# A two-stage attention and FFN kernel: another release of the warm-up matmuls, and one transpose moved from TensorE to DMA

## The chip, the cores and the metric

The kernel runs on one core of one Trainium2 chip. The metric is the device time of one execution in microseconds (us). Three executions of the kernel before lie within 0.4% (317.28 to 318.57 us), so the question here is one of a few microseconds in 318. A profile is one execution of the same program; its span is some 2 us shorter than the time of the run it belongs to (315.7 against 317.68 us before).

## The reference, cut to what matters

```python
def _attn_ref(q, k, v):                      # 8 batches, 8 heads, 576 positions, 64 per head
    q_s = np.exp(q - q.max(-1, keepdims=True));  q_s = q_s / (q_s.sum(-1, keepdims=True) + 1e-09)
    k_s = np.exp(k - k.max(2, keepdims=True));   k_s = k_s / (k_s.sum(2, keepdims=True) + 1e-09)
    kv = np.einsum('bhsd,bhse->bhde', k_s, v)
    return np.einsum('bhsd,bhde->bhse', q_s, kv)

def _moe_ref(x, w_gate, w_val, w_out):       # x: 4608 x 512, d_ff = 1536
    g = x @ w_gate
    silu = g * (1.0 / (1.0 + np.exp(-g)))
    return (silu * (x @ w_val)) @ w_out
```

## The kernel before

All of it is one program with a list of instructions for each engine. The heads of a batch come in two groups, G = 0 and 1. The scaled q of a group must be transposed before the x matmuls (q times kv). There are two ways in the kernel: nine matmuls against an identity and two evictions, or one DMA transpose (the crossbar).

```python
def turn_pe(b, G, i):                        # TensorE: into a PSUM tile
    ...
    for t in range(t0, t1):
        nc.tensor.transpose(out=tp[:, ...], in_=s["qs"][:, t, :], identity=ident)

def turn_out(b, G, i, eng):                  # and out of it again, on ScalarE or VectorE
    copy(eng, s["qt"][:, t0:t1, :], s["tp", i]...)

def turn_dma(b, G):                          # DMA transpose, SyncE queue
    qt = s["qt"] = at.tile([128, T, 128], BF16, tag="qt", name="qt")
    nc.sync.dma_start_transpose(out=qt, in_=s["qs"].rearrange("p t c -> p (t c)"))
```

Batches 0 and 1 use TensorE, batches 2 to 7 the DMA transpose. The program starts with idle matmuls (`spin`) on zeros, only to keep TensorE busy. Then come batch 0's attention, its FFN units (`m_unit`), batch 1's attention with the first four output units (`o_mm`) between its steps, and the FFN in chunks:

```python
spin(9)
spin(7, first)                 # released by the first row sum of q
key_sum(0)
turn_pe(0, 0, 0); turn_pe(0, 0, 1)
...
spin(7)
kv_first(0)                    # needs v, loaded with a cast by a DMA of the GpSimd queue
... [batch 0 continues] ...
load_batch(1, w_dma[-3], by_group=True)      # SyncE queue: q, k, v of 576 KB each, two groups
load_batch(2)                                # right behind it on the same queue
for m in range(MT):
    m_unit(0, S, m, first=(m == 0))
... [exp of q and k, cast of v, sums of batch 1] ...
o_out(0, o_mm(0), nc.scalar)
o_out(1, o_mm(1), nc.scalar)
exp_of("k", 1, 1)
turn_pe(1, 0, 0); turn_pe(1, 0, 1)
turn_out(1, 0, 0, nc.scalar); turn_out(1, 0, 1, nc.scalar)
kv_one(1, 0)
scale_one(1, 0, (nc.vector, nc.vector))
norm_mul(1, 1)
p = o_mm(2)
x_one(1, 0)
o_out(2, p)
turn_pe(1, 1, 0); ...          # group 1 the same way, with o_mm(3)
```

The softmax here doesn't subtract the row's maximum and nothing guards it: scores larger than these inputs give would overflow.

## Time and profile before

| | before |
|---|---|
| time, median of 3 runs | 318.06 us (317.28 to 318.57) |
| span of the profiled run | 315.7 us |
| TensorE busy | 309.0 us, 98% |
| first FFN matmul of batch 0 | 15.40 us |
| first output unit (batch 1's attention begins) | 38.93 us |
| first FFN matmul of chunk 0 (batch 1's attention is done) | 53.11 us |

These are lines of the profile's page. A digit is the busy share of a fortieth of the span in tenths; PE is TensorE, PEld its weight loads, PEclk its granted clock, DVE VectorE, ACT ScalarE, POOL GpSimd.

```profile
PE 309.0 (98%) x1900; PEld 153.0 (48%) x1900; DVE 163.1 (52%) x277; ACT 147.5 (47%) x218; POOL 28.8 (9%) x36
PE   7999999999999999999999999999999999999994
PEclk9999999999999999999999999999999999999998
DMA  7999999179246808490639253944310202020124
```

TensorE has hardly a hole. DMA is full (the digit 9, busy for 90% or more) in the slices from 8 to 55 us: weights, then the loads of batches 1 and 2. What TensorE waited for in the whole span, by the list of waits (total, times, longest):

```profile
PE idle L388 <- DVE sel L367: 1.2, 1, 1.2
PE idle L388 <- DVE rs L138: 1.0, 1, 1.0
PE g_ps L298 <- ACT xt L111: 0.2, 1, 0.2
```

The start, from the timeline of TensorE (start, length, what, count, and in brackets the idle time before it and what ended it):

```profile
1.22 4.02 PE L388 MATMUL idle<-zero 128*128 128x512 bf16 x9 [1.22 <-DVE sel L367]
6.29 3.17 PE L388 MATMUL idle<-zero 128*128 128x512 bf16 x7 [1.05 <-DVE rs L138]
9.25 0.43 PE L397 MATMUL ks<-sel,ek 128*128 128x2 bf16 x9
13.67 0.68 PE L410 MATMUL kv<-v,ek 64*128 64x128 bf16 x18
15.40 0.45 PE L298 MATMUL g_ps<-xt,wg 128*128 128x320 bf16 x2
```

The seven idle matmuls before the key sums take 3.17 us: they start 0.43 us apart. Seven later ones, from 10.25 us, took 1.67 us: 0.22 us apart. These are called the slow and the fast pace here. The view by windows gives a granted clock of 1.00 in every microsecond from 1 to 12 us, so its column does not show this difference. The attention of batch 1, same view:

```profile
44.36 0.68 PE L166 MATMUL tp<-ident,qs 128*128 128x128 bf16 x9
45.60 2.76 PE L322 MATMUL o_ps<-wo,hr 128*128 128x512 bf16 x12
48.30 0.44 PE L220 MATMUL xp<-qt,kn 64*64 64x320 bf16 x8
50.04 2.76 PE L322 MATMUL o_ps<-wo,hr 128*128 128x512 bf16 x12
53.11 0.55 PE L298 MATMUL g_ps<-xt,wg 128*128 128x448 bf16 x2
```

Each of the two output units shown takes 2.7 us; the x matmuls follow without a wait. The twelve DMA transposes of later batches, by the view of the transposed tile:

```profile
L182 SPq DMA_TRANSPOSE qt<-qs x12: 1250/1338/1415, 61.9 to 221.0; - x12
DMA to landing us min/median/max: 3.2/3.3/4.4
```

### The profile page before, as it was taken

The numbers are of one execution on the slowest core, as the hardware profiler recorded it, in microseconds if no ns is written. First come the engines' busy times: TensorE is split into PE (matmuls) and PEld (weight loads), VectorE is DVE, ScalarE is ACT, GpSimd is POOL, SyncE is SP. The second block draws the span as 40 slices with busy tenths as digits, with TensorE's granted clock in tenths as the row PEclk, the third lists the DMA queues.
The fourth block names the chain that finished last, engine by engine and source line by source line (L and its number), as shares of the span: only waits on it lengthen the run. The fifth ranks groups of instructions, "written<-read, shape, count | busy, mean of one in ns | idle before, by whom it ended". The sixth has DMA issues, their size and how long they took to land.

```text
span 315.7 us, 4898 instructions
## 1 busy us (share of the span) xinstructions
PE 309.0 (98%) x1900; PEld 153.0 (48%) x1900; DVE 163.1 (52%) x277; ACT 147.5 (47%) x218; POOL 28.8 (9%) x36
## 2 busy tenths in 40 slices
PE   7999999999999999999999999999999999999994
PEld 2577744554444444544454444544444444444443
DVE  3744476684754566455835492639354333423421
ACT  5653487634673475447454637355743113312300
POOL 2930021101100020002000200020000000000000
PEclk9999999999999999999999999999999999999998
DMA  7999999179246808490639253944310202020124
GB/s 281 182 202 205 298 394 390 60 169 356 55 86 177 341 18 127 125 387 7 141 71 363 83 110 67 323 161 104 67 39 0 52 17 66 0 69 4 30 69 102
DMA packets 40088, 45.75 MB, mean 145 GB/s; under 512 B 17408, under 2 KB 23808, under 8 KB 40064
## 3 DMA queue, kind: packets, MB, share of 16 engines
q1 hardware_dynamic: 32480, 39.99, 42.4%
q0 software_dynamic: 7424, 5.31, 11.2%
q8 instruction: 15, 0.25, 0.3%
q10 hardware_dynamic: 160, 0.13, 0.2%
q14 instruction: 9, 0.07, 0.1%
HBM read 37.75 MB, written 9.44 MB: 149 GB/s over the span
## 4 chain that ended last, share of the span: by engine, by line
PE 94%; ACT 1%; DVE 1%; DMA 1%; issue 0%
PE g_ps L298 30%; PE u_ps L298 29%; PE o_ps L322 27%; PE kv L191 3%; PE idle L388 2%; DMA q<-in_q_dram 1%; PE xp L267 1%; PE tp L166 1%; PE o_ps L342 1%; DVE rs L138 1%; ACT eq L124 1%; PE xp L220 0%; DVE qs L152 0%; ACT L124 0%; PE kv L410 0%
## 5 line engine op out<-in xcount | busy, mean ns | idle before, releaser
L305 ACT ACTIVATE sg<-g_ps 128x512 bf16<-128x512 f32 (+2 forms) x120 | 65.0, 554 | 138.3 <-PE g_ps L298 131.2
L306 DVE TENSOR_TENSOR hr<-sg,u_ps 128x512 bf16<-128x512 bf16 (+2 forms) x120 | 74.4, 630 | 87.2 <-PE u_ps L298 82.3
L298 PE MATMUL g_ps<-xt,wg 128*128 128x512 bf16 (+2 forms) x480 | 111.8, 358 | 0.2 <-ACT xt L111 0.2
L298 PE MATMUL u_ps<-xt,wv 128*128 128x512 bf16 (+2 forms) x480 | 111.5, 358 | 0.0
L322 PE MATMUL o_ps<-wo,hr 128*128 128x512 bf16 x420 | 93.6, 379 | 0.0
L298 PEld LDWEIGHTS <-wv 128*128 128x128 bf16 x480 | 47.0, 98 | 46.4
L298 PEld LDWEIGHTS <-wg 128*128 128x128 bf16 x480 | 45.8, 98 | 45.1 <-issue 0.9
L322 PEld LDWEIGHTS <-hr 128*128 128x128 bf16 x420 | 40.9, 98 | 49.1
L113 DVE COPY o_sb<-o_ps 128x512 f32<-128x512 f32 x33 | 22.4, 680 | 39.2 <-PE o_ps L322 39.2
L127 POOL CAST vb<-v 128x1152 bf16<-128x1152 f32 x14 | 16.0, 1146 | 172.7 <-DMA v<-in_v_dram 113.4
L138 DVE TENSOR_REDUCE rs<-eq 128x18 f32<-128x1152 bf16 (+2 forms) x18 | 21.7, 1215 | 12.8 <-ACT eq L124 12.8
L152 DVE TENSOR_TENSOR qs<-eq,rr 128x1152 bf16<-128x1152 bf16 (+2 forms) x18 | 22.1, 1238 | 0.1
L124 ACT ACTIVATE eq<-q 128x1152 bf16<-128x1152 f32 (+2 forms) x18 | 18.1, 1051 | 4.1 <-DMA q<-in_q_dram 4.0
L124 ACT ACTIVATE ek<-k 128x1152 bf16<-128x1152 f32 x16 | 18.0, 1158 | 0.3 <-DMA k<-in_k_dram 0.2
L305 ACT ACT_TABLE_LOAD x12 | 15.4, 1283 | 0.2
L124 ACT ACT_TABLE_LOAD x11 | 14.1, 1283 | 0.2
L388 PE MATMUL idle<-zero 128*128 128x512 bf16 x26 | 9.7, 534 | 2.3 <-DVE sel L367 1.2
L191 PE MATMUL kv<-vb,ek 64*128 64x129 bf16 x252 | 8.7, 217 | 0.0
L191 PEld LDWEIGHTS <-ek 64*128 64x128 bf16 x252 | 7.3, 94 | 2.7 <-ACT sg L305 2.1
L275 ACT CAST xt<-xp 128x512 bf16<-128x512 f32 x12 | 6.4, 588 | 3.6 <-PE xp L267 3.6
L276 DVE CAST xt<-xp 128x512 bf16<-128x512 f32 x12 | 7.7, 683 | 0.0
L347 ACT COPY o_sb<-o_ps 128x128 f32<-128x128 f32 x2 | 0.5, 265 | 13.3 <-DVE o_sb L346 13.3
(44 smaller groups left out, 72.1 us busy)
## 6 DMA issues: line engine op xcount, KB each, us to landing
q<-in_q_dram SPq DMA_DIRECT2D x16, 576.0 KB, 5.2
k<-in_k_dram SPq DMA_DIRECT2D x16, 576.0 KB, 7.1
out_dram<-o_sb SPq DMA_DIRECT2D x70, 128.0 KB, 2.3
v<-in_v_dram SPq DMA_DIRECT2D x14, 576.0 KB, 8.8
wo<-in_moe_w_out_dram POOLq DMA_DIRECT2D x4, 384.0 KB, 15.3
wg<-in_moe_w_gate_dram POOLq DMA_DIRECT2D x3, 384.0 KB, 11.5
wv<-in_moe_w_val_dram POOLq DMA_DIRECT2D x3, 384.0 KB, 12.5
v<-in_v_dram POOLq DMA_DIRECT2D x2, 288.0 KB, 5.0
```

The costliest lines, as they stand in the source:

```text
L113: eng.tensor_copy(out=out, in_=in_)
L124: nc.scalar.activation(out=e[:, t0:t1], in_=src[:, t0:t1], func=AF.Exp)
L127: nc.gpsimd.tensor_copy(out=vbs[G][:, :, 0:128].rearrange("p t (h d) -> p t h d", d=64), in_=raw["v", b, G].rearrange("p h (t d) -> p t h ...
L138: i = nc.vector.reduce_sum(out=rs[:, 2 * t0:2 * t1], in_=eq2[:, 2 * t0:2 * t1, :], axis=mybir.AxisListType.X)
L152: nc.vector.tensor_mul(qs[:, t0:t1, :].rearrange("p t (h d) -> p (t h) d", d=64), eq2[:, 2 * t0:2 * t1, :], s["rr"][:, 2 * t0:2 * t1].to_b ...
L191: nc.tensor.matmul(out=kv[g][:, c:c + 129], lhsT=ek_of(b, G, g, t), rhs=vbs[G][r, t, 0:129], start=(t == 0), stop=(t == T - 1),)
L276: nc.vector.tensor_copy(out=xt[:, 2 * G + 1, c0:c0 + 512], in_=main[G][1])
L298: nc.tensor.matmul(out=gu[a][i][:, 0:w_], lhsT=(wg, wv)[a][:, kk, ms], rhs=xt[:, kk, c:c + w_], start=(kk == 0), stop=(kk == KT - 1),)
L305: nc.scalar.activation(out=sg[:, 0:w_], in_=g_ps[:, 0:w_], func=AF.Silu)
L306: nc.vector.tensor_mul(hr[:, m, r:r + w_], sg[:, 0:w_], u_ps[:, 0:w_])
L322: nc.tensor.matmul(out=o_ps, lhsT=hr[:, m, r0:r0 + 128], rhs=wo[:, m, :], start=(m == 0), stop=(m == MT - 1),)
L388: i = nc.tensor.matmul(out=idle, lhsT=zero[:, 0:128], rhs=zero, start=True, stop=True)
```

## The change: its intent and its diff

The intent is to bring TensorE to its fast pace sooner and to take nine transposes off TensorE and two evictions off ScalarE in batch 1, where everything waits on a chain. The transpose goes on ScalarE's DMA queue, because the SyncE queue is full of loads (in the profile before they run until about 55 us), and the x matmuls that need it move back by some steps.

```diff
-        spin(9)
-        spin(7, first)
+        spin(10)
+        for i in (0, 2, 4):          # steps: exp, exp, sum, sum, reciprocal of the first q
+            spin(3, steps[i])
 ...
-        spin(7)
+        spin(8)
 ...
         o_out(0, o_mm(0), nc.scalar)
+        turn_dma(1, 0, nc.scalar)
         o_out(1, o_mm(1), nc.scalar)
+        kv_one(1, 0)
         exp_of("k", 1, 1)
-        turn_pe(1, 0, 0)
-        turn_pe(1, 0, 1)
-        turn_out(1, 0, 0, nc.scalar)
-        turn_out(1, 0, 1, nc.scalar)
-        kv_one(1, 0)
-        scale_one(1, 0, (nc.vector, nc.vector))
         norm_mul(1, 1)
+        scale_one(1, 0, (nc.scalar, nc.scalar))
         p = o_mm(2)
-        x_one(1, 0)
-        o_out(2, p)
         turn_pe(1, 1, 0)
         ...
         kv_one(1, 1)
         scale_one(1, 1, (nc.vector, nc.vector))
+        x_one(1, 0)
+        o_out(2, p)
         p = o_mm(3)
```

(`exp_of` and `norm_sum` return their instructions, `turn_dma` takes an engine.)

More of the change, by code (lines that the diff above doesn't have):

```diff
@@ L122, in exp_of @@
         src = raw[what, b, G].rearrange("p h (t d) -> p t h d", d=64)
-        for t0, t1 in pieces:
-            nc.scalar.activation(out=e[:, t0:t1], in_=src[:, t0:t1], func=AF.Exp)
+        return [
+            nc.scalar.activation(out=e[:, t0:t1], in_=src[:, t0:t1], func=AF.Exp) for t0, t1 in pieces
+        ]
     def cast_v(b, G):
@@ L135, in norm_sum @@
         rs = at.tile([128, 2 * T], FP32, tag="rs", name="rs")
-        first = None
-        for t0, t1 in pieces:
-            i = nc.vector.reduce_sum(
+        done = [
+            nc.vector.reduce_sum(
                 out=rs[:, 2 * t0:2 * t1], in_=eq2[:, 2 * t0:2 * t1, :], axis=mybir.AxisListType.X
             )
-            first = first or i
+            for t0, t1 in pieces
+        ]
         rr = s["rr"] = at.tile([128, 2 * T], FP32, tag="rr", name="rr")
-        nc.vector.reciprocal(out=rr, in_=rs)
-        return first
+        done.append(nc.vector.reciprocal(out=rr, in_=rs))
+        return done
     def norm_mul(b, G, pieces=((0, T),)):
@@ L177, in turn_out, with turn_dma @@
         )
-    def turn_dma(b, G):
+    def turn_dma(b, G, eng=nc.sync):
         s = st[b, G]
         qt = s["qt"] = at.tile([128, T, 128], BF16, tag="qt", name="qt")
-        nc.sync.dma_start_transpose(out=qt, in_=s["qs"].rearrange("p t c -> p (t c)"))
+        eng.dma_start_transpose(out=qt, in_=s["qs"].rearrange("p t c -> p (t c)"))
     def ek_of(b, G, g, t):
@@ L371 @@
             nc.vector.memset(vb[:, :, 128:129], 1.0)
-        exp_of("q", 0, 0, BANKS)
+        steps = exp_of("q", 0, 0, BANKS)
         exp_of("k", 0, 0)
         exp_of("q", 0, 1, BANKS)
-        first = norm_sum(0, 0, BANKS)
+        steps += norm_sum(0, 0, BANKS)
         norm_mul(0, 0, BANKS)
```

## The prediction

> **What bounds the kernel.** TensorE. The page gives PE 309.0 us of a 315.7 us span (98%) and 94% of the chain of waits; the wait list names only 2.4 us of PE waiting, all before 54 us. So a gain can only come from PE work removed or from the first 54 us. Two places are bound otherwise: 5 to 39 us, where DMA runs at 90% or more, and 39 to 54 us (batch 1), where the chain passes through exp, sum and multiply of q.
>
> **Part 1, warm-up.** Before: nine idle matmuls from 1.22 us, start to start 0.427 us, then 1.05 us of idle PE, then seven more, still 0.427 us; fast ones (0.216 us) only from about 9.3 us. [...] After: 10+3+3+3, released at about 5.4, 6.2 and 7.1 us, leave no gap above about 0.3 us, so I expect fast matmuls from 5 to 8 us and key sums at about 7.9 instead of 9.25 us. The first FFN matmul then comes 0.5 to 1 us earlier than 15.40. But the weights do not: the third value-weight slice lands at about 22.2 us (read from the POOL issue that waits for it), and before uses it at 22.43. Most of the advance is given back in the fourth FFN unit as a new PE wait on DMA. Gain: 0.2 us, plus perhaps 0.2 in executions whose warm-up phase is bad.
>
> **Part 2, batch 1.** Removed: nine PE transposes (0.68 us), two ScalarE evictions (1.18 us); PE also need not wait 0.2 us for the scaled q at 44.3. Added on ScalarE: the issue of a DMA transpose (1.34 us by the twelve on SP) and two scalings (about 0.35 us each) moved from VectorE. Scaled q of group 1 is ready at about 47.5, its keys at 48.0. PE would reach the first x matmul of group 0 at about 48.9 us. The transpose is issued at about 45.0 us. Alone it lands 3.3 us after issue (48.3): then all is hidden, FFN chunk 0 starts 0.7 us sooner. But DMA is full (390 GB/s) until 55 us with loads of batches 1 and 2. [...] in this trace at 35.2 to 37 us, two queues shared and the older one's rest took about 3 times as long. A transpose is 1152 packets of 256 B, 1.45 us of transfer alone; shared with 2304 B packets I estimate 3 to 8 us, so landing at 49.5 to 55 us: PE would idle 0.5 to 6 us before the x matmuls, possibly followed by slow-clock matmuls. About 45% that it is hidden, 55% that it stalls.
>
> **Sum.** Hidden: -1 us. Stalled: 0 to +5 us. Predicted 318.3 us, 80% range 316.4 to 322.5; faster by over 2%: 1%, within: 94%, slower: 5%.
>
> **To check.** Warm-up: idle matmuls 0.216 us apart before 8 us; wait list with PE on the value weights at 21 to 22 us. Batch 1: x matmuls of group 0 wait for the DMA writing qt, or not; time from transpose issue to landing, 3.3 us or above 5; start of FFN chunk 0 against 53.11 us; ScalarE 1.3 us without work at 45 us.
>
> **What would make it wrong.** A transpose that lands late enough for the clock to fall; q, k loads of batch 2 pushed later by the transpose so that their exp delays the first silu (57.24 us); weight loads landing elsewhere than I read.

The sum came to -1 us if the transpose is hidden and 0 to +5 us if it stalls, together 318.3 us. Two terms stand as estimates alone: that a start without gaps brings the fast pace by 5 us, and that the transpose takes 3 to 8 us beside the loads.

## The result, and the profile after

The changed kernel takes 326.88 us (326.55 to 328.27, 4 runs) against 318.0 us: slower, ratio 1.0289, 95% interval 1.0253 to 1.0325. Ratios here are the mean time of one kernel's fast runs over that of the other's of the same rounds, so not quite the ratio of the medians quoted. The results are correct.

What TensorE waited for, in the changed kernel (two waits of 0.2 us left out):

```profile
PE xp L221 <- DMA qt<-qs: 7.7, 1, 7.7
PE idle L389 <- DVE sel L368: 1.2, 1, 1.2
PE tp L167 <- DVE qs L153: 0.8, 1, 0.8
PE kv L192 <- POOL vb L128: 0.3, 1, 0.3
```

A wait of 7.7 us is new: the x matmuls wait for the DMA that writes the transposed q. Its issue and landing in the view of that tile (ACTq is ScalarE's sequencer; the maximum of the landing times belongs to this one):

```profile
L183 ACTq DMA_TRANSPOSE qt<-qs x1: 1371/1371/1371, 43.9 to 43.9; - x1
DMA to landing us min/median/max: 3.2/3.3/12.7
```

12.7 us instead of 3.3. TensorE's timeline:

```profile
43.77 2.76 PE L323 MATMUL o_ps<-wo,hr 128*128 128x512 bf16 x11
47.30 0.68 PE L167 MATMUL tp<-ident,qs 128*128 128x128 bf16 x9 [0.77 <-DVE qs L153]
48.30 0.70 PE L192 MATMUL kv<-vb,ek 64*128 64x129 bf16 x18 [0.33 <-POOL vb L128]
56.69 0.69 PE L221 MATMUL xp<-qt,kn 64*64 64x320 bf16 x8 [7.69 <-DMA qt<-qs]
57.32 4.43 PE L323 MATMUL o_ps<-wo,hr 128*128 128x512 bf16 x12
62.05 0.55 PE L299 MATMUL g_ps<-xt,wg 128*128 128x448 bf16 x2
```

After the wait, the same output unit takes 4.4 us instead of 2.7. The view by windows gives the reason: the column before the last two is the granted clock.

```profile
48.00:52.00 4.00, 0.70 (x18) 0.62 (x18) 0.94 (x4) 1.05 (x2) 0.25 (x1) 0.81 1.12 324
52.00:56.00 4.00, 0.00 (x0) 0.00 (x0) 0.00 (x0) 0.00 (x0) 0.96 (x1) 0.50 1.06 382
56.00:60.00 4.00, 3.31 (x15) 1.22 (x15) 1.42 (x3) 2.79 (x4) 1.33 (x2) 0.50 0.13 44
```

The granted clock fell from 1.00 to 0.50 in the stall and stayed there for the first work behind it (in narrower windows: from 50.5 to 60.7 us). The last column, GB/s, shows that DMA was busy through the stall, with one dip (230 GB/s from 49 to 50 us), and then nearly idle.

Now the ledger. From the first output unit to FFN chunk 0, before took 53.11 - 38.93 = 14.18 us, and the changed kernel 62.05 - 37.86 = 24.19 us: 10.0 us more. The wait for the transpose is 7.7 of them, the two small waits 1.1, the slow output unit (61.68 - 57.32 against 52.74 - 50.04) 1.7; the removed transposes give 0.6 back. The start, on the other hand, was faster by 15.40 - 14.33 = 1.07 us:

```profile
1.22 6.87 PE L389 MATMUL idle<-zero 128*128 128x512 bf16 x19 [1.22 <-DVE sel L368]
7.93 0.37 PE L398 MATMUL ks<-sel,ek 128*128 128x2 bf16 x9
12.60 0.68 PE L411 MATMUL kv<-v,ek 64*128 64x128 bf16 x18
14.33 0.45 PE L299 MATMUL g_ps<-xt,wg 128*128 128x320 bf16 x2
```

10.0 - 1.07 is 8.9 us, and the spans differ by 324.6 - 315.7 = 8.9 us. So all of the loss is made by 62 us, and nothing later matters.

Why was the transpose late? These are the DMA queues between 52 and 54 us (packets, MB, share of the 16 engines' time). q1 carries the loads of the SyncE queue, q10 the transpose:

```profile
q1 hardware_dynamic: 326, 0.71, 90.5%
q10 hardware_dynamic: 321, 0.08, 18.1%
```

In this window the two queues sent packets one for one (326 to 321), although a load packet has 2304 bytes and a transpose packet 256. The transpose has 1152 packets. At 160 packets per us it needs over 7 us (in the trace 7.9, from 48.0 to 55.9 us), where it takes about 1.5 us alone (before, the first one of batch 2, from 63.2 to 64.7 us). And until about 47.9 us, 4.0 us after its issue, hardly a packet of it was sent at all (2 in the microsecond from 47 us).

### The profile page after: what moved, and what is told of

Read it like the earlier page. It is cut to its first block, busy times and chain, and to the rows that moved or that the text cites. A ratio compares the mean times of both kernels' runs of the same rounds, so it can differ in the third digit from the quotient of the medians.

```text
span 324.6 us, 4858 instructions
## 1 busy us (share of the span) xinstructions
PE 308.6 (95%) x1866; PEld 152.9 (47%) x1895; DVE 162.7 (50%) x275; ACT 147.1 (45%) x218; POOL 29.9 (9%) x36
## 4 chain that ended last, share of the span: by engine, by line
PE 78%; DMA 15%; DVE 2%; ACT 1%; issue 1%; POOL 1%; SPq 1%; DVEq 0%
PE g_ps L299 25%; PE u_ps L299 24%; PE o_ps L323 24%; DMA wo<-in_moe_w_out_dram 5%; DMA qt<-qs 4%; DMA q<-in_q_dram 3%; PE kv L192 2%; DMA wv<-in_moe_w_val_dram 2%; DMA k<-in_k_dram 2%; PE xp L268 1%; DVE rs L138 1%; PE o_ps L343 1%; ACT eq L124 1%; SPq L77 1%; POOL v L360 0%
## 5 line engine op out<-in xcount | busy, mean ns | idle before, releaser
L299 PE MATMUL g_ps<-xt,wg 128*128 128x512 bf16 (+2 forms) x469 | 110.2, 357 | 0.9 <-ACT xt L111 0.2
L299 PE MATMUL u_ps<-xt,wv 128*128 128x512 bf16 (+2 forms) x468 | 110.0, 357 | 0.6
L323 PE MATMUL o_ps<-wo,hr 128*128 128x512 bf16 x415 | 94.8, 384 | 0.2
L128 POOL CAST vb<-v 128x1152 bf16<-128x1152 f32 x14 | 17.1, 1223 | 180.3 <-DMA v<-in_v_dram 148.7
L113 DVE CAST xt<-xp 128x128 bf16<-128x128 f32 (+2 forms) x14 | 5.0, 377 | 11.0 <-PE xp L221 11.0
L111 ACT CAST xt<-xp 128x128 bf16<-128x128 f32 (+2 forms) x14 | 4.6, 350 | 11.1 <-PE xp L221 11.1
L221 PE MATMUL xp<-qt,kn 64*64 64x320 bf16 (+1 forms) x32 | 2.0, 330 | 7.7 <-DMA qt<-qs 7.7
```

The costliest lines, as they stand in the source:

```text
L111: nc.scalar.copy(out=out, in_=in_)
L113: eng.tensor_copy(out=out, in_=in_)
L128: nc.gpsimd.tensor_copy(out=vbs[G][:, :, 0:128].rearrange("p t (h d) -> p t h d", d=64), in_=raw["v", b, G].rearrange("p h (t d) -> p t h ...
L299: nc.tensor.matmul(out=gu[a][i][:, 0:w_], lhsT=(wg, wv)[a][:, kk, ms], rhs=xt[:, kk, c:c + w_], start=(kk == 0), stop=(kk == KT - 1),)
L323: nc.tensor.matmul(out=o_ps, lhsT=hr[:, m, r0:r0 + 128], rhs=wo[:, m, :], start=(m == 0), stop=(m == MT - 1),)
```

## The experiments

Theory A says that the transpose is late because its packets share the engines with those of the loads. The rivals: the new order itself costs the time (B); a transpose is slow at this point whatever runs beside it (C); ScalarE's DMA queue is slow (D); the queues share by bytes, or the transpose waits until the loads end (E).

### The two parts apart

e1 is the changed kernel with batch 1 as before; e2 is the changed kernel with the old warm-up.

```diff
 e1:  all lines from o_out(0, ...) to p = o_mm(3) as before
 e2:  spin(9); spin(7, steps[2]); ... spin(7)        # the old warm-up
```

> Only the warm-up part of the change; batch 1 as before. Theory A (the loss is all in batch 1, the warm-up part gains): first FFN matmul about 1.07 us earlier than before's 15.40, total about 317 us, ratio to before 0.997 (0.995 to 0.999). Rival (the earlier start only runs into weight loads, as I predicted): first FFN matmul earlier, but a PE wait on the value weights near 21 us and a ratio of 0.999 to 1.000.

> Only the batch 1 part; warm-up as before. Theory A: about 10 us slower than before (328 us, ratio 1.031), with the transpose landing 11 to 13 us after its issue and PE waiting 7 to 8 us for qt. If instead the loss came from the two parts meeting, the ratio would stay below 1.02.

e1 took 317.58 us, ratio 0.9987 (0.9972 to 1.0001). Because that interval touches 1, it was timed once more in five rounds:

> The same kernel as e1, timed on the same chip as e10 and with more rounds, to settle whether the warm-up part alone gains: expected ratio 0.997 to 0.9995; key sums at 7.9 us, the first FFN matmul 1.7 us after the second v load has landed.

Ratio 0.9985 (0.9968 to 1.0002). The two agree on about 0.4 us, and neither shows it clear of noise. e2: 328.2 us, ratio 1.0323 (1.0305 to 1.0341), with a wait of 7.72 us for qt. So the batch 1 part alone makes the loss, as theory A has it.

Both rows of expectations on the start hold in part. In e1 the predicted wait on the value weights shows:

```profile
PE u_ps L299 <- DMA wv<-in_moe_w_val_dram: 0.5, 1, 0.5
```

and in e13 another limit does, the load of v:

```profile
7.95 0.37 PE L398 MATMUL ks<-sel,ek 128*128 128x2 bf16 x9
13.95 0.68 PE L411 MATMUL kv<-v,ek 64*128 64x128 bf16 x18 [0.92 <-DMA v<-in_v_dram]
15.68 0.45 PE L299 MATMUL g_ps<-xt,wg 128*128 128x320 bf16 x2
```

In all twelve profiles with the new warm-up (the changed kernel and every experiment but e2) the key sums began between 7.82 and 7.96 us. But the first FFN matmul came anywhere from 14.33 to 17.65 us; ten of the twelve name a wait of 0.5 to 1.8 us for v. In those ten the warm-up no longer is what the start waits for. And the old warm-up is not always slow: e2 has it, and its key sums began at 7.93 us, not 9.25. So the 1.3 us between the profiles before and after cannot be put down to the new warm-up.

### The order without the DMA transpose

e3 puts the TensorE transposes of group 0 where the changed kernel issues the DMA.

```diff
-        turn_dma(1, 0, nc.scalar)
+        turn_pe(1, 0, 0); turn_pe(1, 0, 1)
+        turn_out(1, 0, 0, nc.scalar); turn_out(1, 0, 1, nc.scalar)
```

> The whole change but for the crossbar: group 0 of batch 1 is turned on PE, at the place where the changed kernel issues its DMA transpose, all other steps in the new order. Theory A (the DMA transpose alone costs the time): about 317 to 318 us, ratio 0.996 to 1.000, no wait above 1.5 us in batch 1. Rival B (the new order itself stalls PE): several us slower than before.

322.06 us, ratio 1.013 (1.0097 to 1.0162). This missed what theory A expected, but it was a badly built control. The changed kernel issues the DMA from ScalarE's list; here the TensorE transposes stood at the head of TensorE's list, and their input was not ready for 3.4 us:

```profile
45.57 0.68 PE L167 MATMUL tp<-ident,qs 128*128 128x128 bf16 x9 [3.41 <-DVE qs L153]
46.08 4.44 PE L323 MATMUL o_ps<-wo,hr 128*128 128x512 bf16 x12
```

The output unit behind the 3.4 us wait ran slow here too, 4.4 us instead of 2.7 (the mean granted clock of this execution is 0.992, against 0.997 before). e11 repaired the control: the same transposes, behind `kv_one(1, 0)`.

> A better placed control for e3: the changed kernel without the crossbar, the PE transposes of group 0 placed behind the second output unit and the key-value matmuls, when the scaled q is ready. If only e3's place made it slow: no PE wait above 1 us in batch 1, ratio 0.997 to 1.001. If the new order itself costs: 1.005 or more.

317.92 us, ratio 0.9994 (0.997 to 1.0017), no wait over 0.3 us in batch 1. The new order, together with the new warm-up, costs no time that these runs can tell from noise (at most 0.2%); rival B falls.

### The transpose with and without loads beside it

e4 issues the transpose on the SyncE queue between the loads of batch 1 and those of batch 2. e5 keeps it on ScalarE's queue and makes batch 2's loads wait for it. e12 only swaps the queue, so the transpose stands behind all the loads.

```diff
 e4:     norm_mul(1, 0)
+        turn_dma(1, 0)                  # SyncE queue
+        load_batch(2)                   # moved here from behind load_batch(1, ...)
         ...
-        turn_dma(1, 0, nc.scalar)
 e5:
-        load_batch(2)                   # behind load_batch(1, ...)
-        turn_dma(1, 0, nc.scalar)
+        load_batch(2, turn_dma(1, 0, nc.scalar))     # first load waits until it has landed
 e12:
-        turn_dma(1, 0, nc.scalar)
+        turn_dma(1, 0)
```

> As the changed kernel, but the transpose goes on the queue of the loads, after those of batch 1 and ahead of those of batch 2, so that no load packets run beside it except the tail of batch 1. Theory A (late because it shares the DMA engines one packet for one with 2304-byte load packets): lands 3 to 5 us after issue, before PE asks for it, no stall, ratio to before 0.995 to 0.999. Rival C (a transpose of this tensor at this point is slow whatever runs beside it): still lands 10 us or more after issue, ratio above 1.02.

> As the changed kernel, the transpose still on the ScalarE queue, but the loads of batch 2 wait until it has landed. Theory A (sharing with load packets): lands 3 to 4.5 us after issue, no wait of PE for qt; the loads then come later, so the exps of batch 2 may hold ScalarE and delay the first FFN unit of the chunk by 1 to 3 us. Rival D (the ScalarE queue itself is slow): lands 10 us or more after issue all the same.

> The changed kernel with only the queue changed: SyncE instead of ScalarE at the same place in the program, so behind all loads of batch 2. Theory A: it now queues behind the loads in order, moves at full rate when its turn comes (about 1.5 us) but lands near 55 to 57 us all the same; PE wait for qt 6 to 8 us, total near 326. If the queue order did not matter: landing 3 to 5 us after issue, no wait.

The transpose in e4, and its time to landing, by the view of the tile over 43 to 47 us:

```profile
L183 SPq DMA_TRANSPOSE qt<-qs x1: 1738/1738/1738, 45.1 to 45.1; - x1
DMA to landing us min/median/max: 3.3/3.3/3.3
```

The same for e5, on ScalarE's queue:

```profile
L183 ACTq DMA_TRANSPOSE qt<-qs x1: 1599/1599/1599, 44.3 to 44.3; - x1
DMA to landing us min/median/max: 4.1/4.1/4.1
```

In neither does TensorE wait for qt. In e5 the packets start some 1.3 us after the issue, not 4. That rules out C and D: same point, same queue, almost no loads beside it, and it is fast. E falls by the queues above: between 52 and 54 us the transpose sent 321 packets while the loads ran, with 0.08 MB against their 0.71. But sharing is not all of the lateness. Of the 12.7 us in the changed kernel, 4.1 passed before the first packet, 7.9 from first to last and 0.7 to the landing; in e5 it was 1.3, 1.9 and 0.9. So sharing makes about 6 us of the delay, and the late start 2.8. The loads cause both, but how they hold back the first packet is not shown. e12 landed 9.5 us after its issue, with a wait of 8.0 us and 328.38 us in one run: behind the loads it is as late as among them (whether its packets then moved at full rate was not looked at).

e5 still took 321.36 us in its one run: the loads of batch 2 came later, their exps held ScalarE, and TensorE waited 2.7 us for evictions of x, as expected. e4 took 318.19 us, ratio 1.0006 (0.9991 to 1.0021), above the range I gave for theory A. The stall is gone, but a wait of 0.8 us for x at the end of batch 1 is new for the same reason (an exp of batch 2 before the eviction), and v was late in the profiled start.

### ScalarE's queue at a quiet time

e6 has batch 1 as before and the two transposes of batch 2 on ScalarE's queue.

```diff
-                        turn_dma(b, 0)              # and the same for group 1
+                        turn_dma(b, 0, nc.scalar)
```

> Batch 1 as before (PE transposes), but the two DMA transposes of batch 2, which run when the DMA engines are nearly idle, are issued on the ScalarE queue instead of the SyncE queue. Theory A: they land 3.2 to 3.5 us after issue, as on SyncE. Rival D (ScalarE queue slow, or slow at its first use): 6 us or more for the first or both.

The first landed after 7.8 us, the second after 3.2 us. The time was not as quiet as I had assumed: loads ran until about 69 us in this run. While they ran, the first transpose, issued at 64.0 us, sent its first packets (20) between 68.0 and 68.5 us, so again 4 us or more after its issue. The second met no loads. That fits A, and the second one speaks against D. But the kernel took 326.35 us (one run, with a start that was 2 us later than usual), for a reason that A doesn't cover. ScalarE's timeline:

```profile
59.46 0.98 ACT L306 ACTIVATE sg<-g_ps 128x448 bf16<-128x448 f32 x2
64.04 1.95 ACTq L183 DMA_TRANSPOSE qt<-qs  x1
66.04 0.98 ACT L306 ACTIVATE sg<-g_ps 128x448 bf16<-128x448 f32 x2 [5.60 <-issue]
70.57 1.32 ACTq L183 DMA_TRANSPOSE qt<-qs  x1
71.99 1.85 ACT L306 ACTIVATE sg<-g_ps 128x448 bf16<-128x448 f32 x4 [4.98 <-issue]
```

As I read it, the DMA issues waited for their input in ScalarE's list, and what stood behind them waited too: the SiLU activations stood still for 5.6 and 5.0 us (2.0 and 1.3 of these are the issue itself), and TensorE then waited 1.7 and 2.3 us for them. That its start was late has a cause in the trace too: after a wait of 1.5 us for v the matmuls from 14.56 us on ran slow. 18 key-value matmuls took 1.14 us (0.68 the time before), and 8 x matmuls, at 17.02 us, 0.69 (0.44 the time before).

### Smaller load packets

e7 splits each load of batch 2 in two, so that its packets have 1152 bytes.

```diff
+            half = T * 32
+            for c in (0, half):     # two DMAs of 288 columns each
+                last = nc.sync.dma_start(out=t_[:, :, c:c + half], in_=...)
```

> As the changed kernel, but each load of batch 2 is split into two of 288 columns, so that its packets are 1152 bytes instead of 2304. Theory A (one packet for one): the 1152 packets of the transpose now take about 72 turns of 47+20 ns per engine, near 5 us instead of 7.6; landing 9.5 to 11 us after issue instead of 12.7, PE wait near 5 to 6 us instead of 7.7, transpose packets near 230 per us instead of 160. Rival E (the two queues share by bytes, or the transpose waits for the loads to end): landing unchanged at 12.7 or later.

The landing came at 10.1 us and the wait fell to 5.7 us, both as A had them, but not for the reason given. Between 50 and 52 us:

```profile
q10 hardware_dynamic: 513, 0.13, 111.5%
q1 hardware_dynamic: 115, 0.12, 23.7%
```

The load queue was short of packets then (115 in 2 us, against 607 in the 2 us before): the list of SyncE's waits names earlier loads (3.0 us on v, 2.3 on q and 0.9 on k between 40 and 60 us) ahead of its issues of loads, so the transpose ran partly alone. And where both were busy (54.5 to 55 us) they sent 91 and 80 packets in half a microsecond, so again about one for one, but no faster than with full packets. My figure of 67 ns for a pair (47+20) was an estimate; it can be worked out from the traces before as half of the 94 ns that a load packet of 2304 bytes takes one of 16 engines at the measured 390 GB/s, and 20 ns for each of 1152 transpose packets moved in 1.45 us. It is refuted as far as this window shows: at 160 pairs per us on 16 engines a pair took some 0.1 us for an engine with either size. The total was 326.5 us in one run. In that window e7 speaks for turns by packet (91 to 80) and against turns by bytes (0.10 to 0.02 MB), but it does not isolate the size.

### The clock

e8 adds idle matmuls just before the x matmuls that wait.

```diff
+        spin(34)
         x_one(1, 0)
```

> As the changed kernel, with 34 idle matmuls (7.3 us at full clock) just before the x matmuls that wait for the transpose. Nothing of the wait is taken away. Theory A (part of the loss is slow clock after the stall): the granted clock stays at full speed, o_mm(3) takes 2.7 us instead of 4.4, total about 2 us less than the changed kernel (near 325 us). If the clock does not matter: same 326.9.

The output unit behind the wait:

```profile
57.98 0.44 PE L221 MATMUL xp<-qt,kn 64*64 64x320 bf16 x8 [0.41 <-DMA qt<-qs]
58.35 2.76 PE L323 MATMUL o_ps<-wo,hr 128*128 128x512 bf16 x12
```

2.76 us again, as before; the mean granted clock of this execution is 0.999, against 0.983 in the changed kernel. From the first output unit (39.41 us) to FFN chunk 0 (61.42 us) it took 22.0 us against 24.2 in the changed kernel, and from the x matmuls that had waited to chunk 0 3.4 us against 5.4. So about 2 us of the loss are the clock's. The total, 326.0 us in one run, shows less than that, because this run's first output unit came 1.55 us later than that of the changed kernel's profile.

### A version that beats both

e10 is e4 with two steps moved, so that ScalarE evicts x before it takes up the second exp of batch 2.

```diff
         turn_pe(1, 1, 0); turn_pe(1, 1, 1)
+        xs = x_mm(1, 0, 0), x_mm(1, 0, 1)
+        o_out(2, p)
         turn_out(...); turn_out(...)
         kv_one(1, 1)
+        x_out(1, 0, 0, xs[0]); x_out(1, 0, 1, xs[1])
         scale_one(1, 1, (nc.vector, nc.vector))
-        x_one(1, 0)
-        o_out(2, p)
         p = o_mm(3)
         exp_of("q", 2, 0)
-        exp_of("q", 2, 1)
         x_one(1, 1)
         o_out(3, p)
+        exp_of("q", 2, 1)
```

> A version meant to beat both kernels: new warm-up, transpose on the queue of the loads ahead of those of batch 2 (as e4), the x matmuls of group 0 issued right behind the PE transposes of group 1, and the second exp of q of batch 2 moved behind the last evictions, so that the 0.8 us wait for xt seen in e4 falls to 0.2. From the start of the first output unit to that of FFN chunk 0: about 13.6 us against 14.2 before and 13.9+0.8 in e4. With the warm-up's 0.4 us: ratio to before 0.996 to 0.999.

317.12 us, ratio 0.9971 (0.9951 to 0.9992): a gain of 0.3%, small but clear of 1. From the first output unit to FFN chunk 0 it took 52.02 - 38.36 = 13.66 us, 0.5 us less than before.

## Why the prediction was wrong, point by point

- **What bounds the kernel, and where a change can act: right.** The whole difference lies before 62 us.
- **Warm-up: the number right, the cause not shown.** Key sums were predicted at 7.9 us and came at 7.93, but e2 reached 7.93 with the old warm-up, so the hit may be luck. That the gap in the warm-up holds the fast pace back was an estimate, and no run shows it: e2 has a gap of 1.5 us, and its seven idle matmuls behind the gap took 1.68 us, the fast pace. I said that most of the advance would be given back to the weights; in the profile of the changed kernel it was not (the first FFN matmul kept its 1.07 us to the first output unit), but over many executions the gain is about 0.4 us, unproven. The weights are one of the limits (0.2 to 0.7 us in e1, e8, e11 and e12), the load of v is the more frequent one. I had read the landing of the third value-weight slice as 22.2 us from a GpSimd issue; the weight tile's own view gives about 21.9 us before (issue 11.64, landing 10.3 us later) and 21.0 us in the changed kernel (issue 11.74, landing 9.3 us later).
- **When TensorE would ask for the transpose: right.** Predicted 48.9 us, measured 56.69 - 7.69 = 49.0.
- **"I estimate 3 to 8 us, so landing at 49.5 to 55 us": this term failed.** That sharing with the load packets stretches the transfer was right, and the estimate's upper end was its honest value: packets one for one (326 to 321 in the changed kernel) need over 7 us, and took 7.9. I spread it down to 3 for a sharing by bytes, for which nothing in the trace spoke. And I left the time to the first packet at what it is on a quiet DMA; it was 4.0 us, against 1.3. Landing: 12.7 us after issue, at 56.65 us, although the issue came at 43.9 us and not at the 45.0 that I had assumed.
- **"About 45% that it is hidden": not supported.** No part of the arithmetic gave a landing before 49 us next to full DMA engines (390 GB/s until 55 us before); it was a hope and not an estimate.
- **"PE would idle 0.5 to 6 us, possibly followed by slow-clock matmuls": mis-sized.** 7.7 us, and the clock, which I named and gave no number, cost about 2 us more. The sum for the stalled case, "0 to +5", became +8.9.

## What to carry to other kernels

A second DMA queue brought no more bandwidth here: from 52 to 54 us of the changed kernel the two queues together moved 0.79 MB, some 395 GB/s, where before, from 48 to 52 us, the loads' queue moved 391 GB/s nearly alone (all but one packet). And a transfer of many small packets beside one of large packets sent only one packet for each large one (321 to 326). Count its packets for each engine, times one pair's time (here 0.1 us), and add a late start (here 4 us), before you rely on it to be hidden. Issue it ahead of the bulk loads instead (e4: landed in 3.3 us, not 12.7), and leave it out of a compute engine's list unless its input is ready there (e6: activations held for 5.6 and 5.0 us).

A stall of TensorE can be paid again in slow matmuls behind it. Behind the stalls of 7.7 us (changed kernel) and 3.4 us (e3) an output unit took 4.4 us instead of 2.7; behind 2.7 us (e5) three sets of four FFN matmuls took 1.36, 1.70 and 1.47 us instead of 0.92; behind 1.5 us (e6) 18 key-value matmuls took 1.14 us instead of 0.68. In the changed kernel the granted clock fell to 0.50 only 1.5 us into the stall (49.0 to 50.5 us). So a short wait is not safe either.

## What these runs measured, and what they leave open

- How the two queues take turns: in what the profile counts as packets, they sent one for one (326 to 321 in 2 us), with 2304 bytes against 256; the share in bytes was 0.71 to 0.08 MB. From 48.0 us on, in steps of 0.2 us, it was 31 to 21, 28 to 29 and 36 to 33, about two of each for an engine, which shows no bursts; but the trace does not keep which engine sent a packet, so turns of several by engines out of step are not excluded.
- What such a turn costs: about 0.1 us for an engine and a pair, an estimate (16 engines over 160 pairs per us), with load packets of 2304 bytes and, in one window of e7, of 1152.
- The late start of a transpose next to running loads: its first packets came about 4 us after issue (issue, then the half microsecond of the first packets: the changed kernel 43.9, 47.5 to 48.0 us; e2 44.3, 48.0 to 48.5; e6 64.0, 68.0 to 68.5; e8 45.0, 49.0 to 49.5), against 1.3 us in e5 (44.3, 45.5 to 46.0). With load packets of half the size it was about the same (e7, 45.6, 49.5 to 50.0), so a fixed number of load packets ahead of it does not explain it. Why is open; no run here separates it.
- How the pace varies: the old warm-up led to key sums at 9.25 us (before) and at 7.93 us (e2); the new one at 7.82 to 7.96 us in twelve profiles. What follows a wait varies too: one of 1.52 us before 14.56 us in e6 was followed by slow matmuls, those of 1.28 us (e3, before 14.12 us) and 1.50 us (e2, before 6.41 us) were not. The granted clock stayed at 0.50 for 10.2 us in the changed kernel (50.5 to 60.7 us). What sets it off and what ends it is open.
